# The last steps before the first exponential: value tiles in one row, copied by two engines, with fewer unread products

## The chip, the cores and the metric

One core of a Trainium2 chip. The metric is device time in microseconds. Each run gives every execution's time and the mean clock granted to TensorE in it, and one profiled execution.

## The reference

Two attention blocks on 2048 tokens with 32 heads of 16: A is full, B is causal with a window of 256. Their outputs lie side by side.

```python
def _A_ref(x, wqkv, wo):                       # B=1, S=2048, D=512, H=32, Dh=16
    q, k, v = ...                              # from x @ wqkv
    scores = jnp.einsum("bhqd,bhkd->bhqk", q, k) * (Dh ** -0.5)
    p = _softmax(scores, axis=-1)
    o = jnp.einsum("bhqk,bhkd->bhqd", p, v)
    return ... @ wo
# _B_ref: the same, with mask 0 <= query - key < 256
return jnp.concatenate([a, b], axis=-1)
```

## The kernel before

ScalarE computes the exponentials, 3 banks of 512 columns at a time: one such group is a *slot*. TensorE multiplies the scores of slot s + 2 while ScalarE works on slot s; VectorE copies, reduces and takes part of the exponentials itself as a polynomial. In the lines of the profile PE is TensorE, ACT ScalarE and DVE VectorE, and L252 is line 252 of the kernel; a bank is one block of 512 columns of sums that TensorE writes, so a slot's exponentials (L599) read 128x1536. The start has to turn x, project keys and queries, and find the largest key value (for a bound on the scores) before slot 0 can begin.

The end of that start (cuts marked):

```python
keys(NPASS - 1)                # last key chunk: product, VectorE's maximum, ScalarE's copy
nv = 4
vb = self.ps.tile([P, SLOT, 512], FP32, name="sps", tag="sps", bufs=2)
for t in range(nv):
    bank = vb[:, t, :] if t < SLOT else tile_("op", 1)[:]
    self.v_mm(0, t, bank, range(NC), (0, HV))            # 4 products of 144 columns
    self.v_evac(0, t, bank, nc.scalar.copy, (0, HV))     # copy to SBUF on ScalarE
    if t == 0:
        self.pad_guard(0, mq)
```

`pad_guard` takes the maximum over the key chunks (VectorE), forms `padneg`, multiplies it (the *guard product*, line 526) and adds the result to the queries `qTa` (VectorE, line 529). No score can be multiplied before that.

```python
def busy(self, bank, n):       # products with the identity that nobody reads
    for _ in range(n):
        self.nc.tensor.matmul(bank, lhsT=self.ident[:], rhs=self.junk, start=True, stop=True)
...
# in scores(slot), ahead of the first scores of a slot of A:
self.busy(sps[:, 0, :], 2 - self.whole)
...
# in run():
for n in range(2):
    self.whole = n - 1         # so 3 unread products in slot 0 and 2 in slot 1
    self.scores(slots[n])
```

## Time and profile before

| | before |
|---|---|
| time, median of 3 executions | 1030.43 us (1028.87 to 1030.47) |
| span of the profiled execution | 1027.8 us |
| ScalarE busy | 993.7 us, 97% |
| guard product starts | 18.15 us |
| first scores start | 20.50 us |
| first exponential starts | 20.93 us |
| unread products, whole kernel | 613 |

### The profile page before, as it was taken

To read this page: it belongs to the slowest core of one execution; us is meant where nothing else is said; L and a number is where in the kernel's file an instruction comes from. 1 tells how busy PE (TensorE), PEld (TensorE's weight loads), DVE (VectorE), ACT (ScalarE), POOL (GpSimd) and SP (SyncE) were. 2 spreads that over 40 slices of the span, in tenths; PEclk is the share of its full clock that TensorE was granted. 3 is DMA by queue.
4 is the path that set the end of the run, shared out by engine and by line. 5 is a ranking of instruction groups with operands and counts; after the bars stand their busy time and mean duration, and the time that the engine had idled before them with its cause. 6 is when DMAs were issued, how large, how long until landed. Compare 5 with 4: busy or idle time off the path is not lost.

```text
span 1027.8 us, 18725 instructions
## 1 busy us (share of the span) xinstructions
PE 918.5 (89%) x7577; PEld 314.1 (31%) x7658; DVE 804.2 (78%) x1032; ACT 993.7 (97%) x763; POOL 20.0 (2%) x100
## 2 busy tenths in 40 slices
PE   7999889899888998988899899899998998998887
PEld 5322222232223322332323332233332333233322
DVE  4532279887968898788888898988898878988874
ACT  5999999989999999999999999999999999999996
POOL 6000000000000000000000000000000000000000
PEclk9999999989999999999999999999999999999999
DMA  7021431212232102221240213123202221230011
GB/s 247 8 81 38 144 111 46 76 61 64 74 88 76 64 21 92 79 74 38 74 117 21 74 63 96 58 75 90 79 20 82 74 90 45 60 107 27 32 34 42
DMA packets 72359, 73.05 MB, mean 71 GB/s; under 512 B 22584, under 2 KB 55888, under 8 KB 72272
## 3 DMA queue, kind: packets, MB, share of 16 engines
q1 hardware_dynamic: 69216, 68.01, 21.4%
q0 software_dynamic: 768, 2.13, 0.5%
q10 hardware_dynamic: 2288, 1.70, 0.5%
q8 instruction: 60, 0.98, 0.4%
q14 instruction: 27, 0.22, 0.1%
HBM read 38.65 MB, written 31.07 MB: 68 GB/s over the span
## 4 chain that ended last, share of the span: by engine, by line
ACT 52%; PE 22%; DVE 14%; issue 10%; DMA 2%; ACTq 0%; DVEq 0%
ACT pT L599 52%; PE sps L572 5%; PE ms L252 4%; PE op L691 4%; PE sps L156 4%; DVE dy L631 3%; DVE dh L642 3%; DVE dh L646 2%; PE sps L581 2%; PE ms L628 2%; DVE pD L652 1%; DMA kTa<-in_A_x_dram 1%; DVE ob L421 1%; DVE osb L772 1%; DMA wk<-in_B_wqkv_dram 1%
## 5 line engine op out<-in xcount | busy, mean ns | idle before, releaser
L599 ACT ACTIVATE pT<-sps 128x1536 bf16<-128x1536 f32 (+2 forms) x747 | 983.6, 1465 | 15.4 <-PE sps L572 10.5
L156 PE MATMUL sps<-ident 128*128 128x512 bf16 x613 | 206.8, 382 | 46.6 <-ACT pT L599 39.1
L572 PE MATMUL sps<-qTa,kTa 32*128 32x512 bf16 (+1 forms) x1868 | 242.8, 378 | 5.8 <-ACT pT L599 0.7
L631 DVE COPY dy<-ms 128x512 f32<-128x512 f32 x240 | 164.2, 684 | 63.2 <-PE ms L628 61.3
L691 PE MATMUL op<-pT,va 128*32 128x512 bf16 (+1 forms) x1868 | 182.3, 382 | 0.0
L642 DVE SCALAR_TENSOR_TENSOR dh<-dy 128x1024 f32<-128x1024 uint16 x120 | 146.4, 1220 | 2.7
L646 DVE SCALAR_TENSOR_TENSOR dh<-dy,dh 128x1024 f32<-128x1024 uint16 x120 | 146.1, 1218 | 1.5
L652 DVE SCALAR_TENSOR_TENSOR pD<-dh,dy 128x1024 uint16<-128x1024 f32 x120 | 145.7, 1214 | 1.1
L572 PEld LDWEIGHTS <-kTa 32*128 32x128 bf16 x1868 | 61.1, 91 | 224.6 <-issue 223.7
L156 PEld LDWEIGHTS <-ident 128*128 128x128 bf16 x613 | 56.4, 96 | 162.0 <-issue 150.4
L628 PE MATMUL ms<-qTa,kTa 32*128 32x512 bf16 (+1 forms) x244 | 91.5, 378 | 14.1 <-DVE ob L421 3.8
L691 PEld LDWEIGHTS <-va 128*32 128x32 bf16 x2112 | 50.0, 93 | 102.1 <-issue 100.7
L581 PE MATMUL sps<-mask,ident 128*128 128x128 bf16 (+1 forms) x640 | 77.8, 248 | 0.0
L572 PE MATMUL sps<-qTb,kTb 32*128 32x384 bf16 (+2 forms) x704 | 58.2, 274 | 13.2 <-ACT pT L599 10.8
L581 PEld LDWEIGHTS <-ident 128*128 128x128 bf16 x640 | 43.4, 97 | 32.2 <-issue 29.8
L772 DVE COPY osb<-op 128x512 f32<-128x512 f32 x62 | 42.6, 687 | 8.2 <-PE op L691 7.8
L270 DVE CAST kst<-ms 128x512 bf16<-128x512 f32 x28 | 19.2, 686 | 33.0 <-PE ms L252 33.0
L345 DVE CAST va<-ms 128x368 bf16<-128x368 f32 (+1 forms) x28 | 11.8, 441 | 34.7 <-PE ms L252 34.7
L252 PE MATMUL ms<-wv,xT 128*128 128x368 bf16 (+2 forms) x163 | 35.2, 313 | 3.4 <-DVE dy L631 1.8
L572 PEld LDWEIGHTS <-kTb 32*128 32x128 bf16 x704 | 25.0, 92 | 38.6 <-issue 35.0
L628 PEld LDWEIGHTS <-kTa 32*128 32x128 bf16 x244 | 22.0, 91 | 47.4 <-issue 46.6
L252 PE MATMUL ms<-xT,wq 128*128 128x512 bf16 x100 | 32.2, 388 | 4.0 <-DVE dy L631 1.6
(106 smaller groups left out, 440.2 us busy)
## 6 DMA issues: line engine op xcount, KB each, us to landing
od<-osb SPq DMA_DIRECT2D x62, 256.0 KB
oc<-od SPq DMA_DIRECT2D x31, 256.0 KB
rb<-rd SPq DMA_DIRECT2D x31, 256.0 KB
kTb<-kd SPq DMA_DIRECT2D x16, 256.0 KB
qTb<-qd SPq DMA_DIRECT2D x16, 256.0 KB
qd<-qs SPq DMA_DIRECT2D x31, 128.0 KB
out_dram<-ob SPq DMA_DIRECT2D x31, 128.0 KB
qTa<-qd SPq DMA_DIRECT2D x15, 256.0 KB
```

The lines of the kernel that those rows point to most:

```text
L156: self.nc.tensor.matmul(bank, lhsT=self.ident[:], rhs=self.junk, start=True, stop=True)
L252: self.nc.tensor.matmul(bank, lhsT=lhs(c), rhs=rhs(c), start=(c == 0), stop=(c == NC - 1))
L572: self.nc.tensor.matmul(sps[:, b, o:o + q1 - q0], lhsT=kT[r, gg, k0:k0 + P], rhs=qT[r, gg, q0:q1], start=(o == jb.subs[0][3]), stop=not jb ...
L581: self.nc.tensor.matmul(sps[:, b, o:o + P * len(kind)], lhsT=self.ident[:], rhs=m, start=False, stop=True, skip_group_check=True)
L599: nc.scalar.activation(out=pT[:, b:e, :n], in_=sps[:, b:e, :n], func=ACT.Exp, scale=LN2 / 128, bias=-127 * LN2)
L628: nc.tensor.matmul(b[:, o:o + q1 - q0], lhsT=kT[r, g % 2, k0:k0 + P], rhs=self.qT[0, p, g // 2][r, g % 2, q0:q1], start=True, stop=True, t ...
L631: nc.vector.tensor_copy(out=y[:, half, :], in_=b[:])
L642: nc.vector.scalar_tensor_tensor(out=st["h"][:], in0=low, scalar=-65536.0, in1=low, op0=ALU.add, op1=ALU.mult)
L646: nc.vector.scalar_tensor_tensor(out=st["h"][:], in0=low, scalar=65536.0 * POLY[1], in1=st["h"][:], op0=ALU.add, op1=ALU.mult)
L652: nc.vector.scalar_tensor_tensor(out=out.bitcast(U16), in0=st["h"][:], scalar=POLY[0] * 2.0 ** -41, in1=flat, op0=ALU.mult, op1=ALU.add)
L691: self.nc.tensor.matmul(op[32 * jb.j:32 * jb.j + 32, q0:q1], lhsT=self.v[jb.inst, kt][:, h * VP:h * VP + 32], rhs=jb.pT[:, o:o + q1 - q0], ...
L772: nc.vector.tensor_copy(out=osb[:], in_=self.op[i, p, g][:])
```

## The change

Its intent: start the exponentials sooner. TensorE should not wait for a copy between two value tiles, ScalarE should have fewer copies ahead of the first exponential, and the unread products that stand on this path should go.

```diff
+        banks = [vb[:, t, :] if t < SLOT else tile_("op", 1)[:] for t in range(nv)]
         for t in range(nv):
-            bank = vb[:, t, :] if t < SLOT else tile_("op", 1)[:]
-            self.v_mm(0, t, bank, range(NC), (0, HV))
-            self.v_evac(0, t, bank, nc.scalar.copy, (0, HV))
+            self.v_mm(0, t, banks[t], range(NC), (0, HV))
             if t == 0:
                 self.pad_guard(0, mq)
+        for t in range(nv):
+            self.v_evac(0, t, banks[t], nc.scalar.copy if t < 2 else nc.vector.tensor_copy,
+                        (0, HV))
...
         for n in range(2):
-            self.whole = n - 1
+            self.whole = 2 - n
             self.scores(slots[n])
```

## The prediction

Passages are cut out of the recorded text, each cut marked: rules and figures about the clock, the banks and the cost of a copy that no trace or run here shows, and in rival (b) the count of how full the array is, with the window that it was taken over. The forecast's sum: 0.64 + 0.75 = 1.39 us on TensorE, less 0.27 us for the wait for VectorE, are 1.12 us, so 1030.43 - 1.12 = 1029.31 us. The 275 to 283 ns are ScalarE's copies of 144 columns (L345), and the two copies in 0.53 us are VectorE's. That two engines may copy from two banks at once was not shown. Rival (b) says that with fewer unread products a spell of half clock comes in the start; its 2.6 us are the three waits measured at 225.8 us and just after, its 15% is the author's estimate alone.

> **What bounds the kernel now.** I read the page first, for the engine that has no slack, then the chain of waits over the first 40 us, then the timeline of each engine between 15 and 24 us, because both hunks of the change lie there, and last the granted clock by windows.
>
> The page, busy shares, chain and two groups:
>
> ```profile
> PE 918.5 (89%) x7577; PEld 314.1 (31%) x7658; DVE 804.2 (78%) x1032; ACT 993.7 (97%) x763; POOL 20.0 (2%) x100
> ...
> ACT 52%; PE 22%; DVE 14%; issue 10%; DMA 2%; ACTq 0%; DVEq 0%
> ...
> L599 ACT ACTIVATE pT<-sps 128x1536 bf16<-128x1536 f32 (+2 forms) x747 | 983.6, 1465 | 15.4 <-PE sps L572 10.5
> L156 PE MATMUL sps<-ident 128*128 128x512 bf16 x613 | 206.8, 382 | 46.6 <-ACT pT L599 39.1
> ```
>
> ScalarE is the bound: 983.6 us of exponentials in a span of 1027.8. Line 156 is the product that nobody reads: 613 of them, and they stood idle 39.1 us waiting for the exponentials, so on TensorE they normally lie in slack. The question is therefore only: when does the first exponential start, and is ScalarE fed without a hole from then on?
>
> The chain of waits, first 40 us (start, length, what):
>
> ```profile
> 16.25 1.29 DVE padmax L489 x2
> ...
> 18.15 0.39 PE ms L526
> 18.54 0.36 PE sps L252 x4
> 18.90 0.02 issue
> 18.92 0.29 ACT va L345
> 19.21 0.04 issue
> 19.26 0.41 PE sps L252 x4
> 19.67 0.25 PE op L252 x4
> 19.92 0.65 PE sps L156 x3
> 20.56 0.35 PE sps L572 x3
> 20.91 0.02 issue
> 20.93 2.80 ACT pT L599 x2
> ```
>
> From 18.54 to 20.56 the path to the first exponential runs through exactly what the change touches: products of value tiles (L252), a ScalarE copy between them (L345), and three unread products (L156) ahead of the first scores (L572).
>
> The timelines of TensorE, VectorE and ScalarE (start, length, engine and line, idle before and its releaser):
>
> ```profile
> 19.26 0.41 PE L252 MATMUL sps<-wv,xT 128*128 128x144 bf16 x4 [0.37 <-ACT va L345]
> 19.50 0.41 PE L252 MATMUL op<-wv,xT 128*128 128x144 bf16 x4
> 19.75 0.81 PE L156 MATMUL sps<-ident 128*128 128x512 bf16 x3
> 20.50 0.39 PE L572 MATMUL sps<-qTa,kTa 32*128 32x512 bf16 x3
> ...
> 18.58 0.75 DVE L529 SCALAR_TENSOR_TENSOR qTa<-qTa,top,ms 128x512 bf16<-128x512 bf16 x1 [0.49 <-PE ms L526]
> ...
> 20.93 29.91 ACT L599 ACTIVATE pT<-sps 128x1536 bf16<-128x1536 f32 x22 [0.70 <-PE sps L572]
> 51.05 90.14 ACT L599 ACTIVATE pT<-sps 128x1536 bf16<-128x1536 f32 x67 [0.21 <-PE sps L572]
> ```
>
> Three things are to be seen. The third value tile waits for the copy of the second, although they are different banks. The other input of the first scores, the query block qTa, is finished by VectorE at 18.58 + 0.75 = 19.33, so 1.17 us before the scores start at 20.50: that is the slack the change can take. And once it has begun, ScalarE runs 89 exponentials with one hole of 0.21 us, to 141 us: a start that is earlier should be kept.
>
> The clock, in windows of 1 us (the seventh number after the busy times is the granted clock):
>
> ```profile
> 224.00:225.00 1.00, 1.00 (x9) 0.30 (x8) 1.00 (x2) 0.66 (x2) 0.00 (x0) 1.00 0.75 279
> 227.00:228.00 1.00, 1.00 (x8) 0.22 (x7) 0.58 (x1) 0.00 (x0) 0.00 (x0) 0.50 0.00 0
> ```
>
> From 225.8 to 232.7 us TensorE ran at half clock, although it had been nearly fully busy. ScalarE waited 1.54, 0.50 and 0.59 us for scores there and just after, 2.6 us in all: one such spell costs more than the whole change can give.
>
> [...] ScalarE's kTa copy (L494) idles 1.35 us until VectorE's maximum over the same bank has ended. [...] the trace has 275 to 283 ns. [...] the trace has two such copies (L345 later on) in 0.53 us, 265 ns each.
>
> **The change part by part.**
>
> Part 1, the order of the value tiles. Before: products of tile 0, its copy, the guard product (L526), then tiles 1 to 3 each with its copy, all copies on ScalarE. After: products of all four in one row with the guard product behind tile 0, then the copies, two on ScalarE and two on VectorE. Nothing is added: 16 products and 4 copies stay. The guard product still starts at 18.15 (it waits for VectorE's padneg, untouched). A 512-column product holds TensorE 0.22 us (three unread products are 0.215 apart), so tile 1 starts near 18.36, not at 18.48, and twelve products at 0.062 us (four in 0.25) end their issue near 19.11; before, it was 19.75. Gain on TensorE: 0.64 us, of which 0.12 + 0.53 are the two waits for copies (18.36 to 18.48, and 18.73 to 19.26).
>
> Part 2, unread products. The count per slot is 2 minus `whole`. It was n - 1, so 3 and 2 for slots 0 and 1; it becomes 2 - n, so 0 and 1. Four of five go. The three ahead of slot 0 cost 20.50 - 19.75 = 0.75 us on the path.
>
> Sum on TensorE alone: 0.64 + 0.75 = 1.39 us, so scores possible at 19.11. But qTa is ready only at 19.33, plus 0.05 us of signal (as from padneg's end at 18.09 to L526's weights at 18.14): scores start at 19.38. Realised: 20.50 - 19.38 = 1.12 us; 0.27 us is lost in the wait for VectorE. First exponential: 19.38 + 0.43 (20.50 to 20.93 before) = 19.81.
>
> The copies must not be later than that. ScalarE's two: if the tracking of waits is by whole tile, as the wait at 19.26 suggests, both wait for the third tile's products, which end near 19.03; copies at 19.07 and 19.32, end 19.60, before 19.81. VectorE's two come behind the qTa operation: 19.33 to near 19.85. They free the score buffer of slot 1 near 19.6, when slot 0's scores are just being issued, so slot 1's single unread product starts near 19.70 and its scores near 20.0; they are needed at 19.81 + 1.35 = 21.16. Slack 0.8 us. VectorE was idle 4.15 us there before, so its two copies are free.
>
> After that each slot follows the exponential before it by the same distances, and everything shifts by 1.12 us to the end: 1030.43 - 1.12 = 1029.31 us, 0.11%.
>
> **The rivals.** (a) The gain is eaten later, by a wait for something with a fixed time, such as a load. Against it: the chain has 2% DMA, all before the first scores, and the query and key copies through DRAM start from events that shift along. For it: VectorE and TensorE hold ScalarE up for 13 us over the run. Result: 1029.4 to 1030.4. (b) The clock. [...] If a spell comes in the start it costs about 2.6 us: 1031.9. [...] I give it 15%. (c) The opposite sign of the same: spells anywhere differ from run to run. The three runs before are 1028.87, 1030.43 and 1030.47, two levels 1.6 us apart; if the higher two had one spell more, a median of the changed kernel could fall in the lower level: about 1027.7. (d) VectorE's copies hold up slot 1's scores: this needs 0.8 us of delay, which nothing shows.
>
> **Range and chances.** Centre 1029.2, a little under the sum because the median before lies in the upper of its two levels. The 1.6 us scatter is larger than the gain, so the range goes from 1027.4 (gain and the lower level) to 1030.8 (no gain and a little scatter). Two per cent would be 20.6 us; nothing here touches a fiftieth of the span: within 2% with 0.99, 0.005 on either side.
>
> **What would show it.** Right: guard product still near 18.15; the twelve value products without a ScalarE wait, ended by 19.2; scores of slot 0 near 19.4 with VectorE's qTa as what ended their wait; first exponential near 19.8; no longer hole up to 140 us; 609 unread products instead of 613; ScalarE's busy time lower by about 0.5 us and VectorE's higher by as much. Wrong: a first exponential later than 20.2, a half clock before 30 us, a hole after the second exponential, or the same first start as before. If the start is 1.1 us earlier and the time is not, (a) or the clock spells took it.

## The result, and the profile after

The changed kernel took 1027.24 us in the median of 4 executions (1026.80 to 1028.74); the kernel before, with a fourth execution, 1029.65 us (1028.13 to 1030.47). The ratio is 0.9981, with a 95% interval of 0.9963 to 0.9998. A ratio is the mean time of one kernel's runs over that of the other's of the same rounds, so it is not quite the ratio of the medians. The gain is then about 2.0 us with 0.2 to 3.8 us allowed: the predicted 1.12 us lies inside, and the centre is above it. All outputs are right.

The page of the changed kernel, in the groups that the prediction showed of before:

```profile
PE 915.1 (89%) x7573; PEld 313.8 (31%) x7654; DVE 804.2 (78%) x1034; ACT 993.1 (97%) x761; POOL 20.0 (2%) x100
...
L599 ACT ACTIVATE pT<-sps 128x1536 bf16<-128x1536 f32 (+2 forms) x747 | 983.5, 1462 | 12.9 <-PE sps L572 7.7
...
L156 PE MATMUL sps<-ident 128*128 128x512 bf16 x609 | 205.1, 381 | 47.3 <-ACT pT L599 39.6
```

The exponentials cost the same (983.5 us). ScalarE's idle time ahead of them fell from 15.4 to 12.9 us. Its waits for scores fell by 2.8 us (10.5 to 7.7), but only 0.43 us of that lie ahead of the first exponential (0.70 to 0.27); 2.4 us lie between 215 and 235 us (3.0 to 0.6), in a spell of half clock that is shown below and is not the change. Four unread products fewer, as the diff says.

The chain of waits of the changed kernel over the start (start, length, what):

```profile
19.02 0.40 PE ms L526
19.43 0.02 issue
19.45 0.76 DVE qTa L529
20.21 0.04 issue
20.25 0.41 PE sps L572 x3
...
20.69 2.80 ACT pT L599 x2
```

The value tiles (L252), their copies (L345) and the unread products (L156) are gone from the path. VectorE's query operation has taken their place: a new wait, as predicted. From guard product to first exponential it is now 20.69 - 19.02 = 1.67 us, against 2.79: 1.12 us less.

The timeline of the changed kernel (start, length, engine and line, idle before and releaser):

```profile
19.25 0.66 PE L252 MATMUL sps<-wv,xT 128*128 128x144 bf16 x8
19.75 0.41 PE L252 MATMUL op<-wv,xT 128*128 128x144 bf16 x4
19.95 0.46 ACT L345 CAST va<-sps 128x144 bf16<-128x144 f32 x2 [0.82 <-PE sps L252]
20.45 0.31 DVE L345 CAST va<-sps 128x144 bf16<-128x144 f32 x1 [0.25 <-ACT va L345]
20.81 0.38 PE L156 MATMUL sps<-ident 128*128 128x512 bf16 x1 [0.17 <-DVE va L345]
50.80 90.14 ACT L599 ACTIVATE pT<-sps 128x1536 bf16<-128x1536 f32 x67 [0.21 <-PE sps L572]
```

The twelve value products run in one row without a copy between them. VectorE's first copy waits for ScalarE's second, and slot 1's unread product waits for VectorE; both waits end well before slot 1 is needed at 22.04. The first 89 exponentials again have a single hole of 0.21 us.

But the absolute start is 20.69 us, only 0.25 us ahead of the 20.93 before, and still the profiled span is 2.5 us shorter. Two spells of half clock explain both. The windows of the kernel before, then of the changed kernel (stretch, length, busy times of the five engines, granted clock, DMA):

```profile
8.60:12.00 3.40, 2.83 (x25) 1.78 (x27) 1.81 (x4) 1.70 (x2) 3.02 (x7) 1.00 1.09 350
...
226.00:229.00 3.00, 2.78 (x12) 0.62 (x11) 2.37 (x6) 1.46 (x2) 0.00 (x0) 0.50 0.00 0
```

```profile
8.60:12.00 3.40, 3.18 (x19) 2.00 (x19) 1.00 (x2) 1.20 (x2) 3.02 (x7) 0.51 1.09 349
...
226.00:229.00 3.00, 2.63 (x19) 0.74 (x17) 2.93 (x7) 2.31 (x3) 0.00 (x0) 1.00 0.07 12
```

In the changed kernel's profile the clock was halved from 8.7 to 12.1 us, before anything that the change touches; its guard product comes 0.88 us later, and the other runs show that this is the spell: with the maxima in the old order, it starts at 18.88 to 19.04 us in the four profiles with a spell in the start and at 17.83 to 18.18 us in the seven without. In the kernel before it was halved from 225.8 to 232.7 us. Subtracting the starts of equal exponentials, one kernel from the other: the changed kernel is ahead by 0.25 us at the first, by 0.18 to 0.25 us at each of the first 153, up to 223 us, by 2.4 us at the 160th, at 233 us, and by 2.47 us at the last. So this profile's 2.5 us are 1.12 (the change) less 0.88 (a spell in the start) plus 2.2 (a spell in the other kernel). A look at one pair of profiles would have ascribed all of it to the change.

### The profile page after: what moved, and what is told of

Same layout as the page of the kernel before. It is cut to its first block, busy times and chain, and to the rows that moved or that the text cites. A ratio compares the mean times of both kernels' runs of the same rounds, so it can differ in the third digit from the quotient of the medians.

```text
span 1025.3 us, 18718 instructions
## 1 busy us (share of the span) xinstructions
PE 915.1 (89%) x7573; PEld 313.8 (31%) x7654; DVE 804.2 (78%) x1034; ACT 993.1 (97%) x761; POOL 20.0 (2%) x100
## 4 chain that ended last, share of the span: by engine, by line
ACT 52%; PE 22%; DVE 14%; issue 10%; POOL 1%; DMA 1%; ACTq 0%; DVEq 0%; POOLq 0%
ACT pT L599 52%; PE sps L572 5%; PE ms L252 4%; PE op L691 4%; PE sps L156 4%; DVE dy L631 3%; DVE dh L642 3%; DVE dh L646 2%; PE sps L581 2%; PE ms L628 2%; DVE pD L652 1%; DVE ob L421 1%; DVE osb L772 1%; DMA wk<-in_B_wqkv_dram 1%; DVE qs L376 0%
## 5 line engine op out<-in xcount | busy, mean ns | idle before, releaser
L599 ACT ACTIVATE pT<-sps 128x1536 bf16<-128x1536 f32 (+2 forms) x747 | 983.5, 1462 | 12.9 <-PE sps L572 7.7
L156 PE MATMUL sps<-ident 128*128 128x512 bf16 x609 | 205.1, 381 | 47.3 <-ACT pT L599 39.6
L156 PEld LDWEIGHTS <-ident 128*128 128x128 bf16 x609 | 56.2, 96 | 161.7 <-issue 150.1
L252 PE MATMUL ms<-wv,xT 128*128 128x368 bf16 (+2 forms) x163 | 35.2, 313 | 3.4 <-DVE dy L631 1.7
L345 DVE CAST va<-ms 128x368 bf16<-128x368 f32 (+1 forms) x28 | 11.8, 441 | 32.8 <-PE ms L252 32.8
L252 PE MATMUL ms<-xT,wq 128*128 128x512 bf16 x100 | 31.7, 382 | 3.9 <-DVE dy L631 1.6
```

The lines of the kernel that those rows point to most:

```text
L252: self.nc.tensor.matmul(bank, lhsT=lhs(c), rhs=rhs(c), start=(c == 0), stop=(c == NC - 1))
L599: nc.scalar.activation(out=pT[:, b:e, :n], in_=sps[:, b:e, :n], func=ACT.Exp, scale=LN2 / 128, bias=-127 * LN2)
```

## The experiments

Theory A: the change moves the first exponential by 1.12 us against the guard product, and everything keeps this to the end; the rest is spells of half clock. Theory B: the change also makes spells rarer. The rivals to the parts of A are given with each run.

Each experiment is read in two ways. First, the distances from the start of the guard product in its profile, which no spell ahead of it can move. Second, the time *at full clock*: over all 120 executions that came with a mean clock I fitted one time for each kernel and one common slope (least squares). The slope is 0.65 +- 0.02 us (+- is one standard error throughout) for each 0.001 of mean clock, with 0.52 us left over in a single execution. It agrees with the spell above: 6.83 us at half clock lower the mean by 0.0033, so 2.2 us.

| kernel | scores after guard, us | first exponential after guard, us | executions | mean clock | median, us (run by run) | at full clock, us |
|---|---|---|---|---|---|---|
| before (own run included) | 2.35 | 2.79 | 50 | 0.9948 | 1029.70 (44), 1029.89 (6) | 1026.88 +- 0.12 |
| changed (three runs) | 1.23 | 1.66 | 16 | 0.9976 | 1027.24, 1026.92, 1026.03 | 1025.43 +- 0.14 |
| order only | 1.72 | 2.16 | 6 | 0.9955 | 1027.99 | 1025.96 +- 0.23 |
| unread products only | 1.70 | 2.14 | 6 | 0.9965 | 1028.13 | 1026.11 +- 0.22 |
| all copies on ScalarE | 1.23 | 1.66 | 6 | 0.9968 | 1027.87 | 1025.64 +- 0.22 |
| one unread product in slot 0 | 1.29 | 1.73 | 6 | 0.9972 | 1027.95 | 1025.77 +- 0.22 |
| eight unread products | 3.00 | 3.44 | 6 | 0.9965 | 1029.35 | 1027.24 +- 0.22 |
| earlier maximum (two runs) | 1.23 | 1.67 | 12 | 0.9965 | 1026.91, 1027.13 | 1024.98 +- 0.16 |
| fillers in B | 1.23 | 1.66 | 6 | 0.9973 | 1035.16 | 1033.71 +- 0.22 |
| fillers and earlier maximum | 1.23 | 1.67 | 6 | 0.9983 | 1034.48 | 1033.17 +- 0.21 |

Of the ratios that are not given below, only that of the last row, 1.0041 (1.0016 to 1.0066), has an interval clear of 1.

**The changed kernel again.** No edit.

> The changed kernel again, unaltered, for more executions. Theory A (the start moves 1.12 us, the rest of the first result, 2.0 us in the mean, is chance of half-clock spells): first exponential 1.66 us after the start of the guard product (before: 2.79), whatever the spells; mean time 1.1 us under the kernel before (0.9989), with executions at a lower mean clock about 1.7 to 2.5 us longer. Theory B (the change also makes spells rarer): a repeatable gain of 2 us or more (0.998) with spells in clearly fewer executions than before.

The distance was 1.665 us, in a profile without the spell in the start (first exponential at 19.84 us absolute). Ratio 0.9981 (0.9964 to 0.9999), the same as the first time. The distance is theory A's. The ratio is B's, though A's 0.9989 lies inside the interval. The execution at a mean clock of 1.000 took 1025.99 us and the one at 0.995 took 1029.21. Of the kernel before in the same rounds, the one at 0.988 took 1034.34.

**The order alone.** The changed kernel with the old count of unread products:

```diff
-            self.whole = 2 - n
+            self.whole = n - 1
```

> Value tiles in one row and copied by two engines, but the old five unread products (3 and 2). Theory A: the row ends its issue 0.98 us after the guard product, three unread products add 0.75, scores at 1.73, first exponential 2.16 us after the guard product (0.63 us earlier than before, 0.50 later than with the whole change): time 0.9994. Rival: with the unread products present the order brings nothing, because the copies had been hidden under them: 2.79 us.

```profile
19.86 0.81 PE L156 MATMUL sps<-ident 128*128 128x512 bf16 x3
20.60 0.39 PE L572 MATMUL sps<-qTa,kTa 32*128 32x512 bf16 x3
21.04 2.79 ACT L599 ACTIVATE pT<-sps 128x1536 bf16<-128x1536 f32 x2 [0.77 <-PE sps L572]
```

With the guard product at 18.88 in this profile, the scores come at 1.72 and the first exponential at 2.16, as expected to 0.01 us. The rival, that the copies had been hidden under the unread products, falls: in this order the three follow the last value product at once, and 0.63 us are won at the first exponential. In this profile 0.54 us of them are lost again at 53 us, where VectorE had waited 0.94 us for a store (kd from kst); the profiles of the kernel before and of the changed one have no such loss there. The ratio, 0.9997 (0.9974 to 1.0020), cannot show 0.6 us: one execution at a mean clock of 0.988 took 1034.34.

**The unread products alone.** The kernel before with the new count:

```diff
-            self.whole = n - 1
+            self.whole = 2 - n
```

> Old order of value tiles, each with its own ScalarE copy, but only 0 and 1 unread products. Theory A: the scores move by the three products, 0.75 us, so they start 1.61 us after the guard product and the first exponential at 2.04 us: 0.75 us earlier than before; time 0.9993. The two halves alone sum to 1.38 us, the whole gives 1.12: the missing 0.26 us is the wait for VectorE's qTa. Rival: ScalarE's last two copies, issued at 1.56 and 1.81 us, now hold the exponential up, and it starts later than 2.1 us.

```profile
20.39 0.41 PE L252 MATMUL op<-wv,xT 128*128 128x144 bf16 x4
20.59 0.28 ACT L345 CAST va<-sps 128x144 bf16<-128x144 f32 x1 [0.50 <-PE sps L252]
20.74 0.39 PE L572 MATMUL sps<-qTa,kTa 32*128 32x512 bf16 x3
20.84 0.28 ACT L345 CAST va<-op 128x144 bf16<-128x144 f32 x1
21.18 2.79 ACT L599 ACTIVATE pT<-sps 128x1536 bf16<-128x1536 f32 x2
```

A miss of 0.10 us: scores at 1.70, not 1.61, and the exponential at 2.14, not 2.04. The rival's threshold of 2.1 was passed, but not for its reason: ScalarE's last copy ends at 21.12, just before the exponential, yet the scores themselves are late by the same 0.10 us. The cause is on TensorE. From the last value product, a full-array product of 144 columns, to the scores, which use 32 rows, it was 0.158 us; between two value products it is 0.062. The step from full-array to 32-row products took 0.10 us more. It is not new weights or another bank: in the kernel before, the first unread product, with both, follows the last value product after 0.063 us. It is there before, too, hidden in what I had read as three unread products: from the third of them to the scores it was 0.312 us, between two of them 0.215. Over the whole trace of the kernel before, the 444 steps from an unread product straight to scores have a median of 0.311 us. So three unread products are worth 3 x 0.215 = 0.645 us, and the measured gain is 2.788 - 2.140 = 0.648.

**All copies on ScalarE.** The changed kernel with the second engine taken out:

```diff
-            self.v_evac(0, t, banks[t], nc.scalar.copy if t < 2 else nc.vector.tensor_copy,
+            self.v_evac(0, t, banks[t], nc.scalar.copy,
```

> The changed kernel, but all four value copies on ScalarE. Theory A: the copies follow each other at 0.18 us from 0.93 us after the guard product, the last starts near 1.46 and leaves ScalarE free near 1.7: first exponential at 1.66 to 1.75 us, within 0.1 us of the changed kernel; the second engine is worth almost nothing. Rival: the copies wait for each other's products and signals at 0.25 to 0.3 us each, and the exponential starts 0.3 us or more later, 1.95 or above.

```profile
19.27 0.39 PE L572 MATMUL sps<-qTa,kTa 32*128 32x512 bf16 x3
19.49 0.32 ACT L345 CAST va<-op 128x144 bf16<-128x144 f32 x1
...
19.71 4.13 ACT L599 ACTIVATE pT<-sps 128x1536 bf16<-128x1536 f32 x3
```

First exponential at 1.664 us, the same as in the changed kernel to some nanoseconds. ScalarE's fourth copy starts before the scores are through. The second engine brings nothing here; it is the row, not the split, that counts.

**One unread product back in slot 0.** This measures how much slack the wait for VectorE leaves on TensorE:

```diff
-            self.whole = 2 - n
+            self.whole = 1
```

> The changed kernel with one unread product put back ahead of slot 0 (1 and 1 in place of 0 and 1). TensorE reaches the scores 1.07 us after the guard product (row's end 0.98 and 0.10 until the first scores), VectorE's qTa allows them at 1.23: slack 0.16 us; one unread product is 0.215 us. Theory A (the wait for VectorE caps the gain): first exponential only 0.06 us later, 1.72 us after the guard product. Rival (TensorE alone sets the start): 0.215 us later, 1.88.

The exponential came at 1.725 us, 0.061 us later, for a product of 0.215 us. So 0.154 us of it fell into the wait for VectorE: the cap exists, and its size is 0.15 us, not the 0.27 of the prediction, because 0.10 us belong to the step to 32-row products.

**Eight unread products.** The dose, doubled on the kernel before (6 in slot 0, 2 in slot 1):

```diff
-            self.whole = n - 1
+            self.whole = 4 * n - 4
```

> The kernel before with the unread products ahead of slot 0 doubled, 6 in place of 3 (slot 1 keeps 2). Theory A: each costs 0.215 us of the way to the first exponential, which so moves from 2.79 to 3.43 us after the guard product; time at full clock 0.65 us over the kernel before. On the spells: if more unread products at the start brought more spells (0 of 34 executions with one or two, or with the old three in the old order removed, fell to a mean clock of 0.990 or below, 4 of 28 with five did), this kernel should show them again, mean clock 0.995 or below; if it is chance, nothing is to be seen.

First exponential at 3.44 us: 0.652 us later for three products. On the spells it does not speak for unread products as their cause: mean clock 0.9965, no execution under 0.994. At full clock it is 0.36 +- 0.25 us over the kernel before, against 0.65 expected; the difference is just over one standard error. This profile had no spell before its last 2 us, as had one of the changed kernel (its third run): spans of 1025.6 and 1023.9 us, so 1.7 us apart, with first exponentials at 21.45 and 19.54. Of 1.91 us at the start, 1.67 are there at the end; the 0.26 us go at 152 us, where a load held up the changed kernel and not this one (see the next section).

**VectorE's maximum earlier.** With the wait for VectorE now on the path, its chain of maxima is the next target. The third key chunk's maximum is taken from the product's bank, ahead of ScalarE's copy, as the fourth's is already:

```diff
-            if c == NPASS - 1:
+            if c >= NPASS - 2:
                 largest(bank)
...
-            if c < NPASS - 1:
+            if c < NPASS - 2:
                 largest(kc)
```

> The changed kernel, with VectorE's maximum of the third key chunk taken from the product's bank before ScalarE's copy of it, as the fourth already is, so that VectorE need not wait for that copy. If VectorE's chain of maxima is now what ends before the first scores, the guard product comes about 0.4 us sooner after the fourth key product, the first exponential with it, and the time at full clock falls by 0.4 us to 1025.2. Rival: ScalarE's copies of the key chunks, now later, hold the guard product or the first exponential up, and nothing is gained.

```profile
15.38 0.68 DVE L489 TENSOR_REDUCE padmax<-ms 128x1 f32<-128x512 f32 x1
16.16 0.69 DVE L489 TENSOR_REDUCE padmax<-op 128x1 f32<-128x512 f32 x1
```

The fourth key chunk's products start at 15.10 in this profile and the guard product at 17.46, 2.36 us later; in the changed kernel it was 16.29 to 19.02, so 2.73. The 0.37 us are won, and what follows up to the first exponential is unchanged. At full clock the two runs give 1024.98 +- 0.16 against 1025.43 +- 0.14.

> The changed kernel with the earlier maximum again, beside the changed kernel on one chip: 0.38 us from the fourth key product to the guard product saved, so 0.3 to 0.4 us less at equal clock than the changed kernel of the same job; below what the scatter lets a median show.

The second run's median, 1027.13 us, lies over that of the changed kernel beside it, 1026.03 us, because its mean clock was 0.9963 against 0.9983. At equal clock the fit puts this version 0.45 +- 0.21 us under the changed one, which no median of six executions can show. That all of it lasts is not shown: between the first run's profile and that of the changed kernel's third run, neither with a spell before its last 5.1 us, the lead is 0.41 us at the first exponential, 0.19 us after the load at 151 us, and 0.06 us at the last exponential.

**Fillers against the spells.** That a lightly filled array brings the spells was a guess of mine; no trace had shown it. If it were so, unread products in the light stretches should prevent them:

```diff
-            if b == 0 and jb.inst == 0:
-                self.busy(sps[:, 0, :], 2 - self.whole)
+            if b == 0:
+                self.busy(sps[:, 0, :], (1 if jb.inst else 2) - self.whole)
```

> The changed kernel with one unread product added to those slots of the second, windowed attention that have no other work (63 more). If the half-clock spells come from stretches in which little of the array is filled, there are fewer of them in the run: mean granted clock from 0.997 to 0.998 or above in nearly all executions, and less scatter. Their price: 63 products of 0.215 us on TensorE, hidden if it has slack there, up to 13 us if it has none. Rival: spells come by chance, the clock's scatter stays as it is, and the time grows.

The rival was right. Ratio 1.0053 (1.0026 to 1.0079); at full clock 8.3 us dearer; mean clock 0.9973 with single executions from 0.993 to 1.000, which is no different from the changed kernel.

```profile
L156 PE MATMUL sps<-ident 128*128 128x512 bf16 x672 | 229.3, 381 | 53.5 <-ACT pT L599 45.0
```

Only 8.3 of the 63 x 0.215 = 13.5 us came through, so by this estimate some of the fillers did lie in slack; B's slots have little of it.

> The two runs before together. If both theories hold and the fillers are hidden: first exponential 0.4 us sooner, clock at 0.998 and above, median near 1026 us, so 1 us under the changed kernel. If the fillers are not hidden: as the run with fillers alone, less 0.4 us.

As its second alternative: 1034.48 us, at full clock 0.5 us under the fillers alone. Its mean clock, 0.9983, is the highest of the six-execution means along with one of the changed kernel's, so that fillers do nothing to the clock is not proved, only that they cost more than they could return.

**The changed kernel a third time, and the kernel before against itself.**

> The changed kernel a third time, for more executions of it and of the kernel before on one chip. Theory A: first exponential again 1.66 us after the guard product, times at equal clock 1.1 to 1.4 us under the kernel before, and over all jobs together no clear difference of the mean clock. Theory B: clock again higher than before's by 0.001 to 0.002, so a mean gain of 2 us again.

Distance 1.662 us. Ratio 0.9968 (0.9943 to 0.9993): the largest of the three, and again with a higher clock, 0.9983.

> The kernel before, unaltered, run in the place of a tested kernel against itself. So far its mean clock is 0.9950 in 33 executions, the changed kernel's 0.9975 in 16, and every tested kernel, even the one with eight unread products (0.9965), is above 0.9950. Theory A' (the place in the order of executions, not the kernel, makes the spells rarer): here it gets a mean clock of 0.9965 or more and a ratio under 1 against itself, 0.998 to 0.999, though its times at equal clock agree. Theory B (the kernel before brings more spells): mean clock again near 0.995, ratio 1.000. First exponential 2.79 us after the guard product in either case.

Ratio 0.9998 (0.9978 to 1.0018), mean clock 0.9955, distance 2.79 us. That is nearer to theory B, but it does not exclude A': in the same job the kernel before, in its own place, had 0.9937. The six executions lie 0.5 us over the other 44 at full clock, which shows what six executions can resolve. Over all runs the kernel before had a mean clock of 0.9948 (50 executions) and the changed one 0.9976 (16): the difference, 0.0028, has a standard error of 0.0006 from the two scatters, and at 0.65 us for 0.001 it is worth 1.8 us of the mean. Seven of the 50 were at 0.990 or below, none of the 16.

That would speak for theory B if nothing but the kernel differed, and the place does. All seven are among the 44 executions in the place of the kernel before; in the place of a tested kernel 1 of 76 fell so low. The 60 of these that are not the changed kernel, the old start and eight unread products among them, have a mean clock of 0.9967 against 0.9947 of the 44. In each of the four jobs their mean is the higher one, by 0.0006 to 0.0022. So 0.0020 +- 0.0006 goes with the place, though most of these kernels carry a part of the change, and only 0.0009 +- 0.0005 is left to the changed kernel over the others. Neither the place nor the kernel is shown to be the cause: the order alone (0.9955) and the unread products alone (0.9965) cannot be told from the kernel before with six executions, and no profile caught an execution below 0.995.

The spells are not spread evenly over the kernel. In the 14 profiles, their last 5.2 us aside, six start at 8.5 to 9.1 us, six at 223.8 to 225.8 us, and one each at 188 and 320 us; three profiles have none. The one near 225 us lasts 6.83 us in both profiles of the kernel before and 3.41 us in the four others. That is a lead for theory B that no run here tests. The cause of the clock's difference stays open.

## Why the prediction was right, and where it was off

- **What bounds the kernel, and that an earlier start is kept.** Right. The changed kernel stayed ahead by 0.18 to 0.25 us from the first exponential to 223 us, until the clock of the other was halved. That all of it is always kept is not: against rival (a) the prediction said that the chain's 2% of DMA lies all before the first scores, and this was misread. By the page, 1% is a load of weights for B, and its end is what TensorE waits for near 152 us, in the kernel before:

```profile
151.52 0.60 PE L252 MATMUL ms<-xT,wk 128*128 128x512 bf16 x2 [0.38 <-DMA wk<-in_B_wqkv_dram]
```

In the 14 profiles this load took from 4.88 to 5.62 us, and from the 97th to the 98th exponential it was 1.35 us (eight unread products, no wait there) to 2.09 us. In the chain of waits the load starts 125.3 to 125.4 us after the first exponential in 13 of the 14 (125.9 us in the order alone), so it shifts along with the start. It is no fixed time, but its scatter is of the size of the gain.

- **Part 1, the order: 0.64 us.** Right: 0.63 us alone (0.10 and 0.53 for the two waits, where 0.12 and 0.53 were predicted). The value row ended its issue 0.98 us after the guard product, predicted 0.96.
- **Part 2, the unread products: 0.75 us.** Mis-sized: 0.65 us. I subtracted two starts and read the result as three products; 0.10 us of it was the step from full-array to 32-row products, which remains.
- **The cap by VectorE.** The step was right and set the result: scores at 1.23 us after the guard product, predicted 1.23, exponential at 1.66, predicted 1.66. The loss in it was 0.15 us, not 0.27, for the reason just given. The parts alone sum to 0.63 + 0.65 = 1.28, the whole is 1.12; the difference is the cap.
- **The copies.** That they are not on the path was right, and so was ScalarE's start, 0.93 us after the guard product. The later times were off: ScalarE's two follow at 0.18 us rather than 0.25, and VectorE's wait for ScalarE's second, so they end 1.9 us after the guard product instead of 1.7. The two engines thus never copied at once here (ScalarE from 19.95 to 20.41 us, VectorE from 20.45), although the banks are different. The 265 ns for one VectorE copy was half of a merged pair; single ones took 300 to 313 ns and started 225 ns apart. ScalarE's copies in a row followed each other at 170 to 176 ns in the changed kernel and with all copies on ScalarE; in these and in the kernel before, each took 275 to 316 ns. Slot 1's unread product waits 0.17 us for them, inside the slack named. ScalarE's busy time fell by 0.6 us, as foretold; VectorE's is 804.2 us both times, so that sign does not stand out.
- **The clock.** Rival (b), a spell brought into the start by fewer products, was not seen: in the profiles with the short start, spells lie at 8.6 to 9.1 us, ahead of the changed part, or from 188 us on. I had called the stretch before the spell at 225.8 us nearly fully busy: in the 3.41 us up to 222.4 us it was so (98%), but in the 3.41 us after that, just before the spell, TensorE was busy for 73%. Rival (c), that spells differ from execution to execution and move the median by more than the change does, is what happened. I underestimated it: I took the scatter for two levels 1.6 us apart, and the kernel before later ranged from 1026.97 to 1035.82 us.
- **The time.** 1029.2 was predicted, 1027.24 measured, beside 1029.65 for the kernel before. As an absolute time this lies 0.16 us below the range of 1027.4 to 1030.8; it lies inside only if the range is moved along with the kernel before, whose median fell by 0.78 us with its fourth execution. That the time came so near was in part luck: the term missing from the sum is the mean clock, which only rival (c) had, as chance, and its 1027.7 came nearest. At full clock the two kernels differ by 1.45 +- 0.18 us, of which 1.12 are shown step by step at the first exponential. The remaining 0.3 us come with the pooling of jobs: with a level for each of the four jobs in the fit (116 executions), the two differ by 1.16 +- 0.18 us, which agrees with the 1.12.

## What to carry to other kernels

Before removing work from the path to the first instruction of the bounding engine, find the other input that it waits for: it caps the gain, and here it told the result to 0.01 us. Read the cost of repeated products from their spacing, not from the distance to whatever follows: here 0.10 us of the step from full-array to 32-row products hid there. When the gain is 0.1% and the same kernel's time moves by 0.9%, most of it with the clock, measure distances inside the trace and regress the times on the granted clock; the single pair of profiles differed by 2.5 us, of which 1.12 were the change. And before a difference of the clock is put down to a kernel, run the old kernel in the new one's place often enough to tell.
